# Forgetting attention and a tanh-shrink MLP on one core: another token order for q and k, and another order of the work around batch 0 and batch 1

## The chip, the cores and the metric

The kernel runs on 1 core of one Trainium2 chip. The metric is the device time of one execution in microseconds (us); lower is better. Times of runs are medians, with the lowest and the highest beside them. A profile is one execution taken by the hardware profiler; its span is the time from the first to the last instruction, which is shorter than the device time.

## What is computed

```python
# q, k, v: (8, 8, 576, 64) float32;  f: (8, 8, 576) float32;  w_in: (512, 2048);  w_out: (2048, 512)
scores = q @ k.T / sqrt(64)                       # for each batch and head
cum    = cumsum(log(clip(f, 1e-4, 1)), axis=-1)
scores = where(causal, -1e9, scores + cum[..., :, None] - cum[..., None, :])
attn   = softmax(scores)                          # with 1e-9 added to the sum
x      = (attn @ v).transpose(0, 2, 1, 3).reshape(4608, 512)
h      = x @ w_in
out    = (h - tanh(h)) @ w_out                    # (4608, 512) float32
```

## The kernel before

**Pairs.** Attention runs over 32 pairs of heads: pair p is batch p // 4, heads 2c and 2c+1 with c = p % 4. For each pair the scores are made transposed (keys in partitions, queries along the free side) in seven tiles, named s0 to s6: s0, s1, s2 of the first head, s3 a small tile for the last 64 tokens of both heads, s4, s5, s6 of the second head. A tile is some matmuls into one of two PSUM buffers (`ps_sc`) and one exponential on ScalarE that writes fp16 (`scores`, L260 on). The values of a pair (`values`, L300: 30 matmuls of 65 columns, then a reciprocal and a multiply on VectorE into `xn`) come one pair later, and `turn` (L324) puts the result transposed into `XR`: for batch 0 by TensorE and an eviction, later by a DMA transpose.

**Decay in the matmul.** QT and KT hold 64 rows of q or k and three rows more, in which the cumulated decay stands as a high and a low fp16 part, so that one matmul over 67 rows gives score plus decay. The three rows are written by DMA from the tiles `cc` and `cqs` (`load_aug`, `const_rows`, on SyncE's queue). For s0 and s1 of the very first pair the kernel doesn't wait for that: the variable `direct` takes 64 rows and adds the decay by two more matmuls with the selectors `pick_k` and `pick_q`.

**The mask.** In batch 0 (`early`) the causal mask is one more matmul per diagonal block (`neg16`, `tri16`, L281). From batch 1 on it is an affine select on GpSimd after the exponential (L297), which the values wait for.

**q and k.** Batches 0 to 2 are loaded by `load_qk` with token 6p+n in partition p (96 partitions), transposed on TensorE (`trans`, six transposes of 96 columns for a pair) into a PSUM buffer, and copied out by VectorE (L248), or ScalarE for the first q (L246). From batch 3 on other code does this with DMA transposes.

**Queues.** All loads go through GpSimd's queue in the order in which they are written; `LOADS[(p, ti)]` puts loads behind tile `ti` of pair p. GpSimd runs its queue in order, masks and load issues alike. Small SBUF copies, transposes and stores go through SyncE. All engines run in the order that the program gives them (`manual_schedule`).

**The MLP.** 9 units of 512 tokens, 32 steps each: 16 of `mlp1` (four matmuls of 512 columns, a tanh on ScalarE, an add on VectorE) and 16 of `mlp2` (four matmuls; every fourth step an eviction and a store). Its PSUM buffers are three (`ps_m`), which the transposes of batch 0 share. Pairs 0 to 3 hold no steps. Pair 4 has 3, pairs 5 to 9 have 7 each, all later ones 8; what is left runs behind the last pair.

**Order of the first pairs.** Written out by hand in BEGIN (pair 0), ORDER (1 to 3) and THEN (4): `s` a score tile, `q0` `k0` `q1` ... the transposes for the pair that many ahead, `va` `vb` the values of each head of the pair before, `x` its turn, `h` three quarters of an mlp1 step's matmuls, a bare number so many matmuls that only keep TensorE busy (`spin`), `go` the place from which the steps are spread. From pair 5 on, q's transposes for the next pair stand behind s0, values and turn behind s1, and k's transposes behind s3.

Of the kernel before, what the change touches and what calls it, by code (L numbers as in the profile page):

```python
# [8 lines left out]
FP32 = mybir.dt.float32  # L9
# [5 lines left out]
PITCH = 640  # L15
# [7 lines left out]
def kernel(  # L23
# [31 lines left out]
    aex = ctx.enter_context(tc.tile_pool(name="aex", bufs=10))  # L55
# [67 lines left out]
    pick_k = cst.tile([P, 512], FP16)  # L123
    pick_q = cst.tile([P, P], FP16)
# [4 lines left out]
    EL = [cst.tile([P, 192], FP16, tag=f"el{i}", name=f"el{i}") for i in range(3)]  # L129
    nc.vector.memset(id16, 0.0)  # L130
# [5 lines left out]
    nc.vector.memset(minus16, -1.0)  # L136
    nc.vector.memset(neg16, 0.0)
    nc.vector.memset(tri16, 0.0)
    nc.gpsimd.affine_select(out=neg16, in_=neg16, compare_op=ALU.not_equal,
# [3 lines left out]
    for i in range(2):  # L143
        nc.vector.memset(KT[i][:, :, S:PITCH], 0.0)
    nc.vector.memset(pick_k, 0.0)
    nc.vector.memset(pick_q, 0.0)
    nc.vector.memset(cqs[NH:P, :], 0.0)
    nc.vector.tensor_scalar(out=lf, in0=lf, scalar1=0.0001, scalar2=1.0,
                            op0=ALU.max, op1=ALU.min)
    nc.scalar.activation(out=lf, in_=lf, func=AF.Ln)  # L150
    nc.vector.memset(pick_k[0:1, :], -1.0)
    nc.vector.memset(pick_q[0:1, :], 1.0)
    first = cst.tile([1, 1], FP32)
    nc.scalar.activation(out=first, in_=lf[0:1, 0:1], func=AF.Exp)
    cum = cst.tile([NH, S], FP32)
# [3 lines left out]
    nc.scalar.activation(out=cq, in_=cum, func=AF.Copy, bias=-SHIFT * inv_qscale, scale=inv_qscale)  # L159
    nc.vector.scalar_tensor_tensor(out=clo, in0=cum, scalar=inv_qscale, in1=chi,  # L160
                                   op0=ALU.mult, op1=ALU.subtract)
    nc.vector.memset(pick_k[NH:NH + 1, :], -1.0)

    def load_aug(b):
        i, h0 = b % 2, b * H
        nc.sync.dma_start(out=KT[i][D:D + 1, :, 0:S], in_=chi[h0:h0 + H, :])
        nc.sync.dma_start(out=QT[i][D + 2:D + 3, :, :], in_=cq[h0:h0 + H, :])
        nc.sync.dma_start(out=KT[i][D + 1:D + 2, :, 0:S], in_=cc[NH + h0:NH + h0 + H, :])

    def const_rows(i):  # L170
        nc.sync.dma_start(out=QT[i][D:D + 2, :, :], in_=minus16)
        nc.sync.dma_start(out=KT[i][D + 2:D + 3, :, 0:S], in_=ones16[0:H, :])

    const_rows(0)
    load_aug(0)
    const_rows(1)
    load_qk(qn, q, 0, 4, H)
    load_qk(kn, k, 0, 4, H)
    for e in EL:
        nc.gpsimd.memset(e, 0.0)  # L180
    for i in range(2):
        nc.gpsimd.memset(vn[i][D:P, NJ - 1, :, :], 0.0)
        nc.gpsimd.memset(vn[i][:, :, :, D:VW], 1.0)
    load_v(0)
# [5 lines left out]
    def load_wout(t0, t1):  # L190
# [3 lines left out]
    LOADS = {(0, 0): [lambda: load_qk(qn, q, 1, 0, 2), lambda: load_qk(kn, k, 1, 0, 2),  # L194
                      lambda: load_win(0, DFF // 2)],
             (0, 3): [lambda: load_qk(qn, q, 1, 2, H), lambda: load_qk(kn, k, 1, 2, H)],
             (1, 0): [lambda: load_v(1)],
             (1, 3): [lambda: load_win(DFF // 2, DFF)],
             (2, 0): [lambda: load_wout(0, NFT // 2)],
             (3, 0): [lambda: load_wout(NFT // 2, NFT)],  # L200
             (NPAIR, 5): [lambda: load_qk(qn, q, 2, 0, H)],
             (NPAIR, 6): [lambda: load_qk(kn, k, 2, 0, H)]}
    for b in range(2, B):
        p0 = (b - 1) * NPAIR
        for n in range(NJ - 1):
            LOADS.setdefault((p0 + 1, n), []).append(lambda b=b, n=n: load_v_block(b, n, 0, H))
        LOADS.setdefault((p0 + 1, 4), []).append(lambda b=b: load_v_rest(b))
        LOADS.setdefault((p0, 0), []).append(lambda b=b: load_aug(b))
# [19 lines left out]
    def trans(b, c, src, dst, early, eng, by_head=False):  # L228
        pn, g3 = S // NT6, NT6 // 2
        if early:  # L230
            t32 = ps_m.tile([P, UW], FP32, tag="m", name="t32")
        else:
            t32 = ps_tr.tile([P, UW], FP32, tag="tr", name="t32")
        t16 = t32.bitcast(FP16)[:, 0:2 * S // 2].rearrange("p (a g n) -> p a g n", a=2, g=g3)
        for a in range(2):
            for g in range(g3):
                nc.tensor.transpose(out=t16[:, a, g, :],  # L237
                                    in_=src[b % 2][:, 2 * c + a, 2 * g:2 * g + 2, :],
                                    identity=id16[0:pn, 0:pn])
        for a0, an in ((0, 1), (1, 1)) if by_head else ((0, 2),):  # L240
            for e in range(2):
                h0 = 2 * c + a0
                to = dst[b % 2][0:D, h0:h0 + an, e:S:2].rearrange("d a (p g) -> d a p g", g=g3)
                of = t16[e * D:(e + 1) * D, a0:a0 + an, :, :].rearrange("d a g p -> d a p g")
                if eng == "A":
                    nc.scalar.activation(out=to, in_=of, func=AF.Copy)  # L246
                else:
                    nc.vector.tensor_copy(out=to, in_=of)  # L248

# [10 lines left out]
    def scores(b, c, ti, early):  # L260
# [7 lines left out]
        for a, j, i0, n, col in TILES[ti]:  # L268
            h = 2 * c + a
            edge = min(P, n) if early and i0 == j * P else 0  # L270
            direct = (b, c) == (0, 0) and ti < 2
            rows = D if direct else D + 3
            nc.tensor.matmul(out=ps[:, col:col + n], lhsT=KT[b % 2][0:rows, h, j * P:(j + 1) * P],  # L273
                             rhs=QT[b % 2][0:rows, h, i0:i0 + n], start=True, stop=not (edge or direct))
            if direct:
                nc.tensor.matmul(out=ps[:, col:col + n], lhsT=cc[:, j * P:(j + 1) * P],
                                 rhs=pick_k[:, 0:n], start=False, stop=False)
                nc.tensor.matmul(out=ps[:, col:col + n], lhsT=pick_q,
                                 rhs=cqs[:, i0:i0 + n], start=False, stop=not edge)
# [44 lines left out]
    def turn(b, c):  # L324
        xn = XN.pop((b, c))
        r0 = b % 4 * S
        if b == 0:
            x32 = ps_m.tile([P, UW], FP32, tag="m", name="x32")
# [4 lines left out]
            if c == NPAIR - 1:  # L333
                nc.vector.tensor_copy(out=XR[:, c, r0:r0 + S], in_=xt)
            else:
                nc.scalar.activation(out=XR[:, c, r0:r0 + S], in_=xt, func=AF.Copy)
# [43 lines left out]
    BEGIN = ["8", "q0", "k0", "3", "q1", "2", "s0", "k1", "s1", "s2", "s4", "s5", "q2", "s6", "s3"]  # L380
    ORDER = ["s0", "va", "s1", "vb", "s2", "k1", "s3", "2", "s4", "x", "s5", "q2", "1", "s6"]
    THEN = ["s0", "va", "vb", "s1", "s2", "h0", "h1", "x", "q1", "s3", "go", "s4", "k1", "s5", "s6"]

    def att_items(p):
# [12 lines left out]
        if p <= NPAIR:  # L397
            for what in BEGIN if p == 0 else ORDER if early else THEN:
# [4 lines left out]
                elif what == "go":  # L403
                    items.append((None, False))
                elif kind in "qk":
                    if early and p + int(arg) > NPAIR:
                        continue
                    first = p == 0 and arg == "0"
                    put(trans, *pairs[p + int(arg)], *((qn, QT) if kind == "q" else (kn, KT)), early,
                        "A" if first and kind == "q" else "V", first)  # L410
                elif kind == "v":
                    put(values, *before, (0,) if arg == "a" else (1,), not early)
                elif kind == "x":
# [6 lines left out]
        for ti in range(len(TILES)):  # L420
# [3 lines left out]
            if ti == 0 and after and after[0] < FAR:  # L424
                put(trans, *after, qn, QT, early, "V")
# [3 lines left out]
            if ti == 3 and after and after[0] < FAR:  # L429
                put(trans, *after, kn, KT, early, "V")  # L430
# [4 lines left out]
    with tc.manual_schedule(engines={PE, mybir.EngineType.Pool, mybir.EngineType.SP, mybir.EngineType.DVE,  # L435
                                     mybir.EngineType.Activation}):
        for p in range(len(pairs) + 1):
            if p == 0:
                load_aug(1)
# [4 lines left out]
            given, n, first = 0, 0, 0  # L444
            for emit, counts in items:
                n += counts
                if emit is None:
                    first = n
            whole, n = n, 0
            for emit, counts in items:  # L450
                if emit is not None:
                    emit()
                n += counts
                while n > first and (given + 1) * (whole - first) <= (n - first) * len(mine):
# [33 lines left out]
```

## Time and profile before

| | us |
|---|---|
| median of 3 runs | 365.0 |
| lowest, highest | 363.95, 365.87 |
| span of the profiled execution | 359.3 |
| the profiled execution's own time | not listed |
| TensorE, VectorE, ScalarE, GpSimd busy | 346.5, 199.1, 221.7, 153.6 |

A line of a group names source line, engine, operation, output and inputs, shapes and count; then busy time and the mean of one in ns; then the engine's idle time before them and what ended it. A line of a timeline or of the chain begins with the start in us and a duration. A line of stretches has the stretch, its length, busy time of PE (matmul), PEld (weight load), DVE (VectorE), ACT (ScalarE) and POOL (GpSimd), each with a count, and then the granted TensorE clock, the DMA share and GB/s. A line of a DMA issue ends with the median time from issue to landing. Busy time of TensorE is modelled at the end of a matmul and overlaps.

### The profile page before, as it was taken

What the parts mean: (1) busy time and instruction counts of PE and PEld (TensorE: products, weight loads), DVE (VectorE), ACT (ScalarE), POOL (GpSimd) and SP (SyncE); (2) the same over time, 40 slices, a digit from 0 to 9 for tenths busy, and PEclk for the clock granted to TensorE, in tenths of its full rate; (3) what the DMA queues carried; (4) which work ended last, traced back from release to release, by engine and by line L of the source; (5) the groups of instructions that cost most, each with busy time, mean ns of one, the idle gap of its engine ahead of it and who ended that gap; (6) DMA issues with size and microseconds to landing.
All of it is one profiled execution on the core that took longest, in us unless ns stands there. A gap on an engine that the chain in (4) does not pass through costs nothing.

```text
span 359.3 us, 7490 instructions
## 1 busy us (share of the span) xinstructions
PE 346.5 (96%) x2792; PEld 190.3 (53%) x2792; DVE 199.1 (55%) x349; ACT 221.7 (62%) x416; POOL 153.6 (43%) x316
## 2 busy tenths in 40 slices
PE   7797899999999999999999999999999999999995
PEld 3475455555555555555557865555555554444442
DVE  8666799448961577157814781378127513802710
ACT  6567676558855785578657865686568734714611
POOL 8932463766276627762776267632222210000000
PEclk9789999999999999999999999999999999999999
DMA  7999999999799999999899969991220021011011
GB/s 118 158 188 187 208 194 80 118 145 161 96 102 151 168 97 76 149 181 112 66 144 153 143 65 147 151 156 35 76 75 16 18 77 61 0 60 58 0 48 71
DMA packets 140632, 38.74 MB, mean 108 GB/s; under 512 B 128004, under 2 KB 134900, under 8 KB 140596
## 3 DMA queue, kind: packets, MB, share of 16 engines
q0 software_dynamic: 92320, 18.36, 66.7%
q1 hardware_dynamic: 48276, 19.90, 29.2%
q8 instruction: 22, 0.36, 0.4%
q14 instruction: 14, 0.11, 0.1%
HBM read 36.85 MB, written 9.44 MB: 129 GB/s over the span
## 4 chain that ended last, share of the span: by engine, by line
PE 89%; DVE 6%; ACT 2%; DMA 1%; issue 1%; ACTq 0%
PE ops L370 35%; PE hps L352 32%; PE ps L273 12%; PE av L308 8%; ACT e L287 1%; DVE gt L362 1%; DVE QT L248 1%; DMA QT<-cqs 1%; PE t L237 1%; DVE xn L320 1%; PE ps L281 1%; DVE KT L248 0%; PE spin L226 0%; DVE cum L156 0%; ACT th L359 0%
## 5 line engine op out<-in xcount | busy, mean ns | idle before, releaser
L352 PE MATMUL hps<-XR,win 128*128 128x512 f16 (+1 forms) x640 | 140.9, 357 | 0.3 <-DVE gt L362 0.2
L370 PE MATMUL ops<-wout,gt 128*128 128x512 f16 x576 | 139.2, 378 | 0.0
L287 ACT ACTIVATE e<-ps 128x512 f16<-128x512 f32 x192 | 111.0, 596 | 39.6 <-PE ps L273 26.2
L362 DVE TENSOR_TENSOR gt<-hps,th 128x512 f16<-128x512 f32 x144 | 98.5, 689 | 58.4 <-ACT th L359 57.2
L297 POOL TENSOR_SCALAR_AFFINE_SELECT e<-e 128x128 f16<-128x128 f16 x168 | 56.6, 338 | 120.8 <-ACT e L287 120.5
L359 ACT ACTIVATE th<-hps 128x512 f32<-128x512 f32 x144 | 86.3, 599 | 33.0 <-PE hps L352 31.3
L352 PEld LDWEIGHTS <-win 128*128 128x128 f16 x640 | 57.9, 97 | 48.6 <-issue 0.7
L273 PE MATMUL ps<-QT,KT 67*128 67x64 f16 (+5 forms) x384 | 77.9, 281 | 3.9 <-ACT e L287 2.1
L370 PEld LDWEIGHTS <-gt 128*128 128x128 f16 x576 | 52.0, 97 | 52.6
L273 PEld LDWEIGHTS <-KT 67*128 67x128 f16 (+1 forms) x384 | 37.7, 99 | 41.2 <-issue 2.8
L374 ACT ACTIVATE ost<-ops 128x512 f32<-128x512 f32 x36 | 21.5, 597 | 54.3 <-PE ops L370 45.3
L318 DVE TENSOR_SCALAR rs<-av 128x10 f32<-128x10 f32 (+1 forms) x33 | 5.4, 163 | 69.3 <-PE av L308 69.3
L308 PEld LDWEIGHTS <-e 128*128 128x128 f16 x896 | 32.8, 98 | 7.5 <-issue 1.7
L308 PE MATMUL av<-vn,e 128*128 128x65 f16 x896 | 34.5, 194 | 1.0 <-DVE xn L320 1.0
L106 POOL DMA_DIRECT2D vn<-in_v_dram x32 | 28.4, 898 | 1.6 <-issue 0.8
L320 DVE TENSOR_TENSOR xn<-av,rs 128x640 f16<-128x640 f32 (+1 forms) x33 | 26.5, 804 | 1.1
L248 DVE COPY KT<-t 64x576 f16<-64x576 f16 (+1 forms) x26 | 19.5, 748 | 4.5 <-PE t L237 4.3
L87 POOL DMA_DIRECT2D qn<-in_q_dram x25 | 21.5, 859 | 0.8 <-issue 0.6
L87 POOL DMA_DIRECT2D kn<-in_k_dram x25 | 21.2, 850 | 1.1 <-issue 0.9
L248 DVE COPY QT<-t 64x576 f16<-64x576 f16 x22 | 17.6, 801 | 6.5 <-PE t L237 6.3
L308 PE MATMUL av<-vn,el 128*128 128x65 f16 x64 | 12.5, 195 | 0.0
L95 DVE COPY KT<-TK 64x1152 f16<-64x1152 f16 x20 | 11.4, 607 | 0.1
(58 smaller groups left out, 127.2 us busy)
## 6 DMA issues: line engine op xcount, KB each, us to landing
out_dram<-ost SPq DMA_DIRECT2D x36, 256.0 KB
vn<-in_v_dram POOLq DMA_DIRECT2D x32, 128.0 KB, 5.9
qn<-in_q_dram POOLq DMA_DIRECT2D x20, 128.0 KB, 3.7
kn<-in_k_dram POOLq DMA_DIRECT2D x20, 128.0 KB, 4.4
win<-in_moe_w_in_dram POOLq DMA_DIRECT2D x2, 1024.0 KB, 11.8
wout<-in_moe_w_out_dram POOLq DMA_DIRECT2D x2, 1024.0 KB, 17.4
XR<-xn SPq DMA_TRANSPOSE x56
qn<-in_q_dram POOLq DMA_DIRECT2D x1, 576.0 KB, 8.9
```

The costliest lines, as they stand in the source:

```text
L87: nc.gpsimd.dma_start(out=dst[b % 2][0:pn, n, :].rearrange("p (h d) -> p h d", h=H), in_=src[b, :, n * P:n * P + pn, :].rearrange("h p d - ...
L106: nc.gpsimd.dma_start(out=vn[b % 2][:, n, h0:h1, 0:D], in_=v[b, h0:h1, n * P:(n + 1) * P, :].rearrange("h p d -> p h d"))
L248: nc.vector.tensor_copy(out=to, in_=of)
L273: nc.tensor.matmul(out=ps[:, col:col + n], lhsT=KT[b % 2][0:rows, h, j * P:(j + 1) * P], rhs=QT[b % 2][0:rows, h, i0:i0 + n], start=True, ...
L287: nc.scalar.activation(out=e[:, lo:hi], in_=ps[:, lo:hi], func=AF.Exp, scale=qscale)
L297: nc.gpsimd.affine_select(out=view, in_=view, compare_op=ALU.is_ge, fill=0.0, base=0, pattern=pat, channel_multiplier=-1)
L308: nc.tensor.matmul(out=av[:, a, ib, :], lhsT=E.pop((b, c, a, j, ib)), rhs=vn[b % 2][:, j, 2 * c + a, 0:D + 1], start=(j == 0), stop=(j == ib))
L320: nc.vector.tensor_tensor(out=xn[:, :, h0 * D:(h0 + hn) * D].rearrange("p i (a d) -> p a i d", a=hn), in0=av[:, h0:h0 + hn, :, 0:D], in1=r ...
L352: nc.tensor.matmul(out=hps[:, o:o + n], lhsT=win[:, ci, ft * P:(ft + 1) * P], rhs=XR[:, ci, t:t + n], start=(ci == 0), stop=(ci == NCH - 1))
L359: nc.scalar.activation(out=th, in_=hps, func=AF.Tanh, scale=-1.0)
L362: nc.vector.tensor_tensor(out=gt, in0=hps, in1=th, op=ALU.add)
L370: nc.tensor.matmul(out=ops, lhsT=GT[(u, ft)][:, m * P:(m + 1) * P], rhs=wout[:, ft, :], start=(ft == 0), stop=(ft == NFT - 1))
```

## The change

Six things are altered.

1. `load_qk` puts token 96n+p into partition p, so it reads pieces of 64 floats where it read 384. `trans` writes QT and KT in runs of 96 neighbouring elements where it wrote every second element.
2. All score tiles of head 0 of batch 0 are `direct`, with one 2-column tile `pick` broadcast as the selector. The DMA rows of decay are written for heads 1 to 7 at first (`const_rows(0, 1, H)`, `load_aug(0, 1)`), and head 0's constant rows in pair 4. The copy of `cq` on ScalarE stands behind the first two evictions of q (`cum_q`).
3. Fills and copies move between engines: the fills of `vn` from GpSimd to VectorE, the turns of batch 0 all to VectorE and to the buffer `ps_tr`, and batch 1's fills and rows into pair 0 (`later_rows`).
4. Loads: batch 0's q and k go in four parts each, v ahead of the last of them. The first-layer weights go in four parts behind them, in pairs 0 and 1. Batch 1's heads 0 to 3 follow in pairs 2 and 3 with the second-layer weights between; batch 1's v is in pair 4 behind s1, heads 4 to 7 of its q and k in pair 4 behind s4, and batch 2's q and k behind s6.
5. The order of pairs 0 to 4 is written in ORDERS. Pairs 1 to 3 have no spins. In pair 4 the values, three `h`, the turn and four steps (`m`) come ahead of batch 1's first transposes and scores; the pair holds 13 steps.
6. Pairs 5 to 8 have 5 steps, later ones 8.

```diff
     def load_qk(dst, src, b, h0, h1):
         nc.gpsimd.dma_start(
-            out=dst[b % 2][:, h0:h1, :, :].rearrange("p h n d -> p h (n d)"),
-            in_=src[b, h0:h1, :, :].rearrange("h (p n) d -> p h (n d)", n=NT6))
+            out=dst[b % 2][:, h0:h1, :, :].rearrange("p h n d -> p (h n) d"),
+            in_=src[b, h0:h1, :, :].rearrange("h s d -> (h s) d").rearrange("(m p) d -> p m d", p=S // NT6))
...
-    LOADS = {(0, 0): [lambda: load_qk(qn, q, 1, 0, 2), lambda: load_qk(kn, k, 1, 0, 2),
-                      lambda: load_win(0, DFF // 2)],
-             (0, 3): [lambda: load_qk(qn, q, 1, 2, H), lambda: load_qk(kn, k, 1, 2, H)],
-             (1, 0): [lambda: load_v(1)],
-             (1, 3): [lambda: load_win(DFF // 2, DFF)],
-             (2, 0): [lambda: load_wout(0, NFT // 2)],
-             (3, 0): [lambda: load_wout(NFT // 2, NFT)],
-             (NPAIR, 5): [lambda: load_qk(qn, q, 2, 0, H)],
-             (NPAIR, 6): [lambda: load_qk(kn, k, 2, 0, H)]}
+    QW = DFF // 4
+    LOADS = {(0, 3): [lambda: load_win(0, QW), lambda: load_win(QW, 2 * QW)],
+             (1, 3): [lambda: load_win(2 * QW, 3 * QW), lambda: load_win(3 * QW, DFF)],
+             (2, 3): [lambda: load_qk(qn, q, 1, 0, 2), lambda: load_qk(kn, k, 1, 0, 2)],
+             (3, 3): [lambda: load_wout(0, NFT // 2), lambda: load_qk(qn, q, 1, 2, 4),
+                      lambda: load_qk(kn, k, 1, 2, 4), lambda: load_wout(NFT // 2, NFT)],
+             (NPAIR, 1): [lambda: load_v(1)],
+             (NPAIR, 4): [lambda: load_qk(qn, q, 1, 4, H), lambda: load_qk(kn, k, 1, 4, H),
+                          lambda: const_rows(0, 0, 1)],
+             (NPAIR, 6): [lambda: load_qk(qn, q, 2, 0, H), lambda: load_qk(kn, k, 2, 0, H)]}
...
-                to = dst[b % 2][0:D, h0:h0 + an, e:S:2].rearrange("d a (p g) -> d a p g", g=g3)
-                of = t16[e * D:(e + 1) * D, a0:a0 + an, :, :].rearrange("d a g p -> d a p g")
+                to = dst[b % 2][0:D, h0:h0 + an, 0:S].rearrange("d a (g e p) -> d a g e p", g=g3, e=2)[:, :, :, e, :]
+                of = t16[e * D:(e + 1) * D, a0:a0 + an, :, :]
...
-            direct = (b, c) == (0, 0) and ti < 2
-            rows = D if direct else D + 3
+            direct = b == 0 and h == 0
...
-    BEGIN = ["8", "q0", "k0", "3", "q1", "2", "s0", "k1", "s1", "s2", "s4", "s5", "q2", "s6", "s3"]
-    ORDER = ["s0", "va", "s1", "vb", "s2", "k1", "s3", "2", "s4", "x", "s5", "q2", "1", "s6"]
-    THEN = ["s0", "va", "vb", "s1", "s2", "h0", "h1", "x", "q1", "s3", "go", "s4", "k1", "s5", "s6"]
+    BEGIN = ["8", "q0", "k0", "3", "s0", "q1", "s1", "k1", "s2", "s4", "s5", "q2", "r", "s6", "s3"]
+    ORDERS = [BEGIN,
+              ["s0", "s1", "k1", "s2", "va", "s3", "vb", "s4", "q2", "s5", "x", "s6"],
+              ["s0", "va", "s1", "vb", "s2", "k1", "s3", "s4", "x", "s5", "s6"],
+              ["s0", "va", "s1", "vb", "s2", "s3", "s4", "x", "s5", "s6"],
+              ["va", "vb", "h0", "h1", "h2", "x", "m", "m", "m", "m", "q0", "m", "k0", "m", "m", "m",
+               "s0", "m", "s1", "m", "q1", "s2", "m", "s3", "m", "k1", "s4", "s5", "m", "s6"]]
...
-            take = 0 if p < NPAIR else 3 if p == NPAIR else 7 if p <= 2 * NPAIR + 1 else 8
+            take = 5 if p <= 2 * NPAIR else 8
```

More of the change, by code (lines that the diff above doesn't have):

```diff
@@ L142 @@
                             fill=BIG, base=0, pattern=[[1, P]], channel_multiplier=-1)
[L143 to L149, printed above, removed]
     nc.scalar.activation(out=lf, in_=lf, func=AF.Ln)
-    nc.vector.memset(pick_k[0:1, :], -1.0)
-    nc.vector.memset(pick_q[0:1, :], 1.0)
     first = cst.tile([1, 1], FP32)
     nc.scalar.activation(out=first, in_=lf[0:1, 0:1], func=AF.Exp)
-    cum = cst.tile([NH, S], FP32)
+    nc.vector.memset(vn[0][D:P, NJ - 1, :, :], 0.0)
+    nc.vector.memset(vn[0][:, :, :, D:VW], 1.0)
     nc.vector.tensor_tensor_scan(out=cum, data0=ones16[0:NH, :], data1=lf, initial=0.0,
@@ L327, in turn @@
         if b == 0:
-            x32 = ps_m.tile([P, UW], FP32, tag="m", name="x32")
+            x32 = ps_tr.tile([P, UW], FP32, tag="tr", name="x32")
             xt = x32.bitcast(FP16)[:, 0:S]
@@ L397, in att_items @@
         if p <= NPAIR:
-            for what in BEGIN if p == 0 else ORDER if early else THEN:
+            for what in ORDERS[p]:
                 kind, arg = what[0], what[1:]
```

126 lines of the change are left out of this document (72 added, 54 removed).

## The prediction

> **What bounds the kernel now.** I read the page first, then the busy time by stretches, then TensorE's timeline and the chain of waits up to 62 us, and last Pool's queue.
>
> ```profile
> PE 346.5 (96%) x2792; PEld 190.3 (53%) x2792; DVE 199.1 (55%) x349; ACT 221.7 (62%) x416; POOL 153.6 (43%) x316
> PEclk9789999999999999999999999999999999999999
> 10.00:15.00 5.00, 3.25 (x31) 2.05 (x30) 3.29 (x5) 2.54 (x5) 5.00 (x8) 0.91 2.07 151
> 15.00:20.00 5.00, 4.53 (x53) 3.68 (x51) 2.12 (x5) 2.29 (x5) 5.00 (x7) 0.50 1.22 164
> 60.00:70.00 10.00, 10.00 (x93) 5.65 (x92) 5.71 (x11) 5.42 (x11) 6.83 (x14) 1.00 0.75 80
> ```
>
> The stretches list PE, PEld, DVE, ACT and POOL busy time, then the granted clock. From 60 us on PE has no idle time; before that it has, and from about 14 to 21 us it ran at half clock. So only two things count: when PE becomes full, and how much PE work is left then. The marks for this are these rows.
>
> ```profile
> 13.21 0.38 PE L273 MATMUL ps<-QT,KT 67*128 67x512 f16 x1
> 16.50 0.58 PE L273 MATMUL ps<-QT,KT 67*128 67x512 f16 x1 [0.47 <-ACT e L287]
> 23.32 0.38 PE L273 MATMUL ps<-QT,KT 67*128 67x512 f16 x1 [0.34 <-ACT e L287]
> 28.24 0.38 PE L273 MATMUL ps<-QT,KT 67*128 67x512 f16 x1 [0.37 <-ACT e L287]
> 33.54 0.47 PE av L308 x15
> 60.47 0.38 PE L273 MATMUL ps<-QT,KT 67*128 67x512 f16 x1
> 69.32 0.38 PE L273 MATMUL ps<-QT,KT 67*128 67x512 f16 x1
> 61.11 0.86 PE ops L370 x4
> 62.20 0.91 PE av L308 x30
> 25.29 0.26 PE t L237 x6
> ```
>
> Pair 1 begins at 16.50, pair 2 at 23.32, pair 3 at 28.24, the values that open pair 4's stretch at 33.54, pair 7 at 60.47, pair 8 at 69.32. An MLP step (four 512-column matmuls) takes 0.865 us, a pair's values 0.91, a set of six transposes 0.26. A full pair with seven steps takes 8.85; a pair with five therefore 8.85 - 2 x 0.865 = 7.12. By 60.47 the old kernel has done pairs 0 to 6 and 3 + 7 + 7 = 17 steps. The whole sum is: when has the new one done as much?
>
> The span is 359.3 us and the median of the runs 365.0. The profiled execution's own time is not listed, so I make the sum on the span and carry the 5.7 us between them over unchanged.
>
> **Part 1, the head and pairs 1 to 3: 2.9 to 5.0 us gained.**
>
> ```profile
> 8.06 4.42 DMA QT<-cqs
> L246 ACT ACTIVATE QT<-t 64x288 f16<-64x288 f16 x4 | 1.9, 484 | 0.0
> L287 ACT ACTIVATE e<-ps 128x512 f16<-128x512 f32 x192 | 111.0, 596 | 39.6 <-PE ps L273 26.2 <-PE ps L281 5.8 <-POOL e L297 5.6
> L287 ACT ACTIVATE el<-ps 128x128 f16<-128x128 f32 x32 | 8.8, 276 | 4.0 <-PE ps L273 3.9 <-PE ps L281 0.2
> L336 ACT ACTIVATE XR<-x 128x576 f16<-128x576 f16 x3 | 1.9, 645 | 0.0
> ```
>
> The old head waits until 12.48 (8.06 + 4.42) for the decay rows that DMA writes, and only then issues the third tile of head 0. With selectors for all of head 0 that tile goes out before. The wait stays for head 1: its row now leaves ACT behind two evictions (2 x 0.484), some 0.65 later, so head 1's first tile moves from 13.21 to about 13.6. But one tile and its exponential (0.6) are already out of the way, and pair 1 begins at 15.7 to 16.0 and not 16.50. The extra selector matmuls (two times 576 columns at 0.865 us for 2048, 0.5 us) lie in the wait for that DMA and cost nothing; 0.5 if that wait were gone.
>
> Pairs 2 and 3 are ACT's: 6 x 0.596 + 0.276 + 0.645 = 4.5 of the 4.92 between 23.32 and 28.24. The XR eviction (0.645) goes to DVE, which leaves 4.25. The taken-out spins lay in ACT's time, so they give nothing themselves. Pair 1 depends on the clock.
>
> ```profile
> 10.80:14.20 3.40, 1.66 (x13) 0.93 (x12) 2.52 (x4) 1.39 (x3) 3.40 (x6) 0.99 2.20 148
> 38.10:41.50 3.40, 1.78 (x16) 1.08 (x16) 2.77 (x5) 1.74 (x5) 0.59 (x2) 1.00 1.24 209
> 12.87 0.30 PE L273 MATMUL ps<-QT,KT 67*128 67x320 f16 x1 [1.34 <-DMA QT<-cqs]
> ```
>
> Pair 1 has 3.5 us of matmuls (scores 1.37, which is 8.85 less seven steps, the values and two sets of transposes; values 0.91, ten masks of 128 columns 0.5, two transposes of 0.26, a turn). At half clock they end at about 22.1; at full clock ACT sets 4.25 like in the others, and they end at 20.0. Two more pairs give 30.6 or 28.5 for the values now at 33.54. I take 29.6, half of the slow stretch kept: the old clock fell after the stretch with 1.66 us of PE in 3.4 and kept through the one with 1.78, and the new head has some 0.4 more than 1.66 between 10.8 and 14.2. At full clock throughout, the time comes out 1.1 lower than forecast, 366.9; a third of the main case.
>
> Here the Trainium skill (TensorE: Matmul & The Clock Gate, "Why this matters for your kernels") says that the clock halves after an idle gap of about 3 us. The trace does not agree: the longest gap before the fall at 14 is 1.34 us. By the page the new head would stay at full clock.
>
> **Part 2, pair 4: 13 steps instead of 3, all PE work that was due anyway.**
>
> ```profile
> L248 DVE COPY QT<-t 64x576 f16<-64x576 f16 x22 | 17.6, 801 | 6.5 <-PE t L237 6.3
> 38.83 0.81 DVE QT L248
> 37.34 0.29 PE x L332 x5
> L334 DVE COPY XR<-x 128x576 f16<-128x576 f16 x1 | 0.5, 458 | 1.1 <-PE x L332 1.1
> L362 DVE TENSOR_TENSOR gt<-hps,th 128x512 f16<-128x512 f32 x144 | 98.5, 689 | 58.4 <-ACT th L359 57.2
> L359 ACT ACTIVATE th<-hps 128x512 f32<-128x512 f32 x144 | 86.3, 599 | 33.0 <-PE hps L352 31.3
> ```
>
> The q and k evictions write with stride 2 now and take 0.801; the XR copy of the same 576 elements, unit stride, takes 0.458. The new order gives unit stride in runs of 96: I take 0.46, with 0.80 as the other end. That shortens the old chain around 38.8 us, which ran over these copies.
>
> From the values of pair 3 to the end of pair 4's scores and pair 5's first tile PE has 0.91 + 13 x 0.865 + four transposes of 0.26 + the turn 0.3 + scores 1.37 and 0.2 of the next pair = 15.1. Idle: 0.6 for the XR copy, 1.2 for the first tanh and gt (0.2 + 0.60 + 0.69, less the two short steps under it), and 1.4 at k0, whose one PSUM buffer is held by q0 until gt (0.69) and two evictions (0.92) are done. Sum 18.3: PE gets to pair 5's q transposes at 29.6 + 18.3 = 47.9. The second tile of pair 4 (s1) ends 13.15 after 29.6, at 42.75.
>
> **Part 3, the load that pair 5 needs: 6.8 us of waiting, the term that decides.** Those transposes read heads 4 to 7 of batch 1's q. Their load stood in pair 0; now it is queued on Pool in pair 4 behind tile s4's mask, and ahead of that, behind s1's mask, stand the five loads of batch 1's v.
>
> ```profile
> L106 POOL DMA_DIRECT2D vn<-in_v_dram x32 | 28.4, 898 | 1.6 <-issue 0.8 <-PE hps L352 0.2 <-PE ops L370 0.2
> L98 POOL DMA_DIRECT2D vn<-in_v_dram x8 | 5.7, 708 | 0.2 <-PE ps L273 0.2
> L297 POOL TENSOR_SCALAR_AFFINE_SELECT e<-e 128x128 f16<-128x128 f16 x112 | 34.0, 304 | 51.3 <-ACT e L287 51.1
> L297 POOL TENSOR_SCALAR_AFFINE_SELECT e<-e 128x256 f16<-128x256 f16 x56 | 22.7, 406 | 69.5 <-ACT e L287 69.5
> qn<-in_q_dram POOLq DMA_DIRECT2D x20, 128.0 KB, 3.7
> qn<-in_q_dram POOLq DMA_DIRECT2D x1, 288.0 KB, 5.1
> kn<-in_k_dram POOLq DMA_DIRECT2D x1, 288.0 KB, 6.6
> DMA to landing us min/median/max: 3.4/4.9/11.9
> ```
>
> s1 ends at 42.75; a tanh ahead of it, its exponential and its mask take 1.55, to 44.3; the v loads hold Pool 4 x 0.898 + 0.708 = 4.3, to 48.6; three masks (0.41 + 0.33 + 0.30) to 49.6. Then the load. The trace has loads of this size (four heads, 288 KB) at 5.1 and 6.6 from issue to landing, and 3.7 as the median of 128 KB; the last row is the fastest, middle and slowest of q's first six loads. I take 5.1, the same tensor and size: landed at 54.7. PE is in order, so nothing behind the transposes moves from 47.9 to 54.7. Queued behind it are all of pair 5's scores and values, and ACT and DVE starve with it. Ends: even with Pool free after s4's own mask, mask and 3.7 us of landing would leave 3.5; with 6.6 it is 8.3. k's load lands two or three microseconds later, when PE is still in pair 5's values and steps, and hides.
>
> **Sum.** From 54.7: the rest of pair 5, 7.12 - 0.22 = 6.9, and pair 6, 7.12, reach 68.7 with 13 + 5 + 5 = 23 steps, six more than 17 (5.2 us of work). So the old mark is reached at 63.5, against 60.47: +3.0. The tail is the same. Forecast 365.0 + 3.0 = 368.0. By the bounds: 28.5 with 3.7 gives +0.5, 30.6 with 6.6 gives +5.5.
>
> Cost nothing: the first-layer weights. Pool issues them at once behind batch 0's loads, at about 15 us.
>
> ```profile
> win<-in_moe_w_in_dram POOLq DMA_DIRECT2D x1, 1024.0 KB, 10.6
> ```
>
> The first half is then there at about 26, needed from 30.5; twice 10.6 is 36, and the fourth quarter is needed at about 46. Lateness would count in full. The later rows of decay for batch 2 on SP are needed three pairs on and cover themselves.
>
> **Rivals.** *The load lands in time (10%).* Then pair 5 runs on at 47.9 and the mark is reached at 56.7: -3.8, 361.2. It decides from a landing less than 2 us after s4's mask; the fastest of those six took 3.4, and Pool's order puts 4.3 us of v issues in front. In its favour: the 18.3 us of pair 4 are worked out by hand, and PE could be late for other reasons that hide the wait.
>
> *Small pieces clog the DMA (12%).* q and k of batches 0 to 2 are read in pieces of 256 bytes and not 1536, six times as many packets.
>
> ```profile
> q0 software_dynamic: 92320, 18.36, 66.7%
> vn<-in_v_dram POOLq DMA_DIRECT2D x4, 128.0 KB, 5.2
> ```
>
> 92,320 packets held 66.7% of 16 engines' 359.3 us: 41.5 ns each. At that price a two-head load of 1152 packets takes 3.0 us, against about 1 now; the second k pair and the first scores of pair 1 would be some 3 us late, and the wait of part 3 2 us longer: 371 to 373. Against it: v blocks already come in such pieces, 1024 packets each, issued 0.9 us apart and landing with the same 5.2, so a packet costs at most 14 ns; packet times overlap.
>
> The Trainium skill (DMA: Bandwidth & Descriptors, "Specifications") wants at least 512 bytes a transfer and sees read-modify-write below it; by it this rival would hold.
>
> *No spins, so the clock falls again in pairs 2 and 3 (5%):* each would then take 6.6 and not 4.25, 372. Against it: 3.3 us of matmuls in 4.25 is more than the 1.78 in 3.4 that kept full clock.
>
> *The evictions stay at 0.80 (7%):* 0.35 more at k0 twice over, and 0.6 in pair 1: about 369.5.
>
> **Numbers.** The main case has 66%, 365.5 to 370.5. 0.5% (1.8 us) is about what a measurement of this kernel can tell. Of the main case some four fifths lie above 366.8; with the slow rivals that is 0.73 slower; 0.17 within; faster is the 10% of the load in time. For eight in ten: 364.8 to 371.0.
>
> **What would show it.** A TensorE wait of 4 to 8 us on the DMA of qn in the first pair after the 13 steps; QT evictions at 0.46; the values of pair 3 at 28.5 to 30.6; Pool's v issues straight ahead of a 288 KB qn load. I am wrong if PE shows no wait of over 2 us on that load, or if the steps before it take over 20 us.

## The result, and the profile after

The changed kernel takes 368.95 us (368.07 to 369.9, 4 runs) beside 364.48 us (363.09 to 365.87, 4 runs) for the kernel before: ratio 1.0135, 95% interval 1.0094 to 1.0177. The forecast was 368.0, that is +3.0; measured is +4.5. The profiled execution took 368.07 us with a span of 366.4, so 1.7 us lie outside the span.

Ratios leave disturbed executions out, so they can differ a little from the quotient of the medians beside them.

The page of the changed kernel: busy time, the granted clock in 40 slices of 9.2 us, the first DMA queue (packets, MB, packet time), and the share of each engine in the chain that ended last.

```profile
PE 346.3 (95%) x2787; PEld 189.6 (52%) x2787; DVE 183.1 (50%) x358; ACT 219.2 (60%) x413; POOL 162.7 (44%) x318
PEclk9899997999999999999999999999999999999999
q0 software_dynamic: 116480, 18.36, 75.3%
PE 89%; DVE 3%; ACT 2%; DMA 2%; POOL 1%; issue 1%; ACTq 0%
```

TensorE is as busy as before (346.5 then), and the span is 7.1 longer. So the difference is idle time, or time at half clock taken for busy time. The clock row has a dent in its second slice, and a deeper one in the seventh, where the old kernel had none. TensorE's timeline shows why (start, duration, instruction, then the idle time before it and what ended it); its first two rows are the first tiles of pairs 1 and 2.

```profile
15.94 0.38 PE L287 MATMUL ps<-QT,KT 67*128 67x512 f16 x1
20.59 0.38 PE L287 MATMUL ps<-QT,KT 67*128 67x512 f16 x1
29.41 0.58 PE L322 MATMUL av<-vn,e 128*128 128x65 f16 x14
31.02 0.58 PE L322 MATMUL av<-vn,e 128*128 128x65 f16 x14 [1.00 <-DVE xn L334]
34.41 0.81 PE L363 MATMUL hps<-XR,win 128*128 128x512 f16 x3 [0.55 <-DVE XR L347]
36.19 1.02 PE L363 MATMUL hps<-XR,win 128*128 128x512 f16 x4 [0.98 <-DVE gt L373]
39.55 0.41 PE L249 MATMUL t<-id,kn 96*128 96x96 f16 x6 [1.21 <-DVE QT L260]
55.38 0.66 PE L249 MATMUL t<-id,qn 96*128 96x96 f16 x6 [5.76 <-DMA qn<-in_q_dram]
56.28 1.90 PE L363 MATMUL hps<-XR,win 128*128 128x512 f16 x4
71.80 0.38 PE L287 MATMUL ps<-QT,KT 67*128 67x512 f16 x1
```

The values of pair 3 come at 29.41, 4.0 earlier than before (33.38 in the old kernel's timeline; the 33.54 of the prediction is from its chain of waits). Then TensorE stands still for 5.76 us on the load of q, and the four matmuls after it take 1.90 us and not 1.02: half clock. Pair 7 begins at 71.80 with 23 steps done. Less the six steps more (5.2, as in the prediction) that is 66.6 against 60.47: +6.1.

On Pool's timeline and in the chain of waits the load is found where it was expected: s1's mask, five loads of v, three masks not shown, the issue, and 5.22 us to its landing.

```profile
44.83 0.29 POOL L311 TENSOR_SCALAR_AFFINE_SELECT e<-e 128x128 f16<-128x128 f16 x1 [0.79 <-ACT e L301]
45.07 3.53 POOL L106 DMA_DIRECT2D vn<-in_v_dram  x4
48.57 0.72 POOL L98 DMA_DIRECT2D vn<-in_v_dram  x1
```
```profile
50.12 5.22 DMA qn<-in_q_dram
```

The stretches around the wait (columns as in the prediction: length, then busy time of PE, PEld, DVE, ACT and POOL, granted clock, DMA, GB/s) give the clock. It falls in the second stretch, while TensorE still waits, and stays at 0.50 for all of the third, although TensorE has no gap there. In finer stretches it is half from about 53.4 to 60.3: 2 us of the wait, and the first 4.9 us of work behind it.

```profile
49.60:53.00 3.40, 0.03 (x1) 0.00 (x0) 0.53 (x1) 0.79 (x2) 3.40 (x7) 1.00 1.67 106
53.00:56.40 3.40, 1.02 (x9) 0.80 (x10) 0.32 (x1) 0.00 (x0) 3.40 (x3) 0.56 2.31 148
56.40:59.80 3.40, 3.40 (x37) 2.27 (x35) 1.28 (x3) 1.20 (x2) 2.53 (x5) 0.50 2.38 152
59.80:63.20 3.40, 3.40 (x24) 1.72 (x22) 2.32 (x5) 2.19 (x5) 0.49 (x2) 0.93 3.23 153
```

The evictions fell as taken (0.46), in the groups by line:

```profile
L260 DVE COPY QT<-t 64x576 f16<-64x576 f16 x22 | 9.9, 452 | 13.6 <-PE t L249 13.5
```

### The profile page after: what moved, and what is told of

Its sections match the earlier page's. It is cut to its first block, busy times and chain, and to the rows that moved or that the text cites. A ratio compares the mean times of both kernels' runs of the same rounds, so it can differ in the third digit from the quotient of the medians.

```text
span 366.4 us, 7488 instructions
## 1 busy us (share of the span) xinstructions
PE 346.3 (95%) x2787; PEld 189.6 (52%) x2787; DVE 183.1 (50%) x358; ACT 219.2 (60%) x413; POOL 162.7 (44%) x318
## 3 DMA queue, kind: packets, MB, share of 16 engines
q1 hardware_dynamic: 48302, 19.90, 27.2%
## 4 chain that ended last, share of the span: by engine, by line
PE 89%; DVE 3%; ACT 2%; DMA 2%; POOL 1%; issue 1%; ACTq 0%
PE ops L381 33%; PE hps L363 33%; PE ps L287 12%; PE av L322 8%; ACT e L301 1%; DMA qn<-in_q_dram 1%; PE t L249 1%; DMA XR<-xn 1%; POOL vn L106 1%; DVE xn L334 1%; ACT th L370 1%; PE ps L295 0%; DVE gt L373 0%; DVE cum L173 0%; PE ps L290 0%
## 5 line engine op out<-in xcount | busy, mean ns | idle before, releaser
L287 PE MATMUL ps<-QT,KT 67*128 67x64 f16 (+4 forms) x384 | 78.6, 279 | 3.6 <-DVE KT L260 1.8
L287 PEld LDWEIGHTS <-KT 67*128 67x128 f16 x384 | 36.8, 98 | 39.2 <-issue 4.2
L260 DVE COPY QT<-t 64x576 f16<-64x576 f16 x22 | 9.9, 452 | 13.6 <-PE t L249 13.5
L260 DVE COPY KT<-t 64x576 f16<-64x576 f16 (+1 forms) x26 | 11.2, 429 | 4.3 <-PE t L249 4.1
L249 PE MATMUL t<-id,qn 96*128 96x96 f16 x72 | 5.8, 224 | 5.8 <-DMA qn<-in_q_dram 5.8
```

The lines of the kernel that those rows point to most:

```text
L287: nc.tensor.matmul(out=ps[:, col:col + n], lhsT=KT[b % 2][0:D + 3, h, j * P:(j + 1) * P], rhs=QT[b % 2][0:D + 3, h, i0:i0 + n], start=True ...
```

## The experiments

My theory after the result: the wait on the load costs its 5.8 us and, through the clock, some 2 us more, and what the rest of the change gains is less than that. The rivals: the small pieces of the new token order hold up the loads; or the selectors and the new order of pair 4 cost the time themselves.

A mark that does without what comes later in an execution is the start of pair 7 in each profile, which all variants of the changed kernel reach with the same 23 steps. In the kernel as changed it is 71.80, and 72.47 in a second profile of it (below), so differences under some 0.7 say little.

**The kernel before, once more** (unaltered).

> The kernel before, once more. In the changed kernel's runs the time lies 1.7 us above the span, so the spans of the old kernel's timed runs (363.1 to 365.9 us) should be 361.4 to 364.2, and its profile of 359.3 an execution from the fast end. Theory: this run has a span of 361 to 364.5, and what it has more than 359.3 is half clock, in another place or longer (the 1.6 us gap at 38 us is the candidate). Rival: span 359 to 360 again and some 5 us outside it, so that the two profiles may be compared as they stand, a difference of 7.1.

Measured: 362.1 us (358.82 to 365.3, 10 runs), ratio 0.9955 (0.9914 to 0.9995); span 360.5. Its waits (in total, times, longest) and its stretches from 14 to 26 us:

```profile
PE ps L273 <- DMA QT<-cqs: 2.5, 1, 2.5
14.00:20.00 6.00, 5.05 (x54) 3.98 (x55) 1.60 (x2) 3.42 (x7) 5.10 (x8) 0.63 1.42 168
20.00:26.00 6.00, 5.66 (x81) 4.29 (x79) 4.31 (x7) 4.02 (x9) 2.12 (x3) 0.81 1.20 198
```

The wait for the rows of decay is 2.5 here and was 1.34 in the profile of the prediction; half clock stands in the same stretch. So the old kernel varies by 2% without any change to it. Its span goes roughly with its mean granted clock: over these 10 executions and 30 more it is 357.1 us at 0.997 and 0.998, 359.3 to 360.5 at 0.988 and 0.990, 360.4 to 361.4 at 0.983, and 362.2 to 364.2 at 0.974. The span of 360.5 is a little under the 361 that I expected, but 1.7 us lie outside it and not the 5 of the rival. The profile that I had built on, 359.3, was near the short end: its time would be about 361.0, and not the 365.0 of the median.

**The load early.** Heads 4 to 7 of batch 1's q and k are loaded with heads 2 and 3, in pair 3.

```diff
-             (3, 3): [lambda: load_wout(0, NFT // 2), lambda: load_qk(qn, q, 1, 2, 4),
-                      lambda: load_qk(kn, k, 1, 2, 4), lambda: load_wout(NFT // 2, NFT)],
+             (3, 3): [lambda: load_wout(0, NFT // 2), lambda: load_qk(qn, q, 1, 2, H),
+                      lambda: load_qk(kn, k, 1, 2, H), lambda: load_wout(NFT // 2, NFT)],
...
-             (NPAIR, 4): [lambda: load_qk(qn, q, 1, 4, H), lambda: load_qk(kn, k, 1, 4, H),
-                          lambda: const_rows(0, 0, 1)],
+             (NPAIR, 4): [lambda: const_rows(0, 0, 1)],
```

> The changed kernel with heads 4 to 7 of batch 1's q and k loaded together with heads 2 and 3, in pair 3, and not behind tile s4 of pair 4. Theory: the 5.8 us wait goes, and the stretch at half clock behind it (some 4.3 us of work at half speed, so 2.1 us) goes with it: 368.9 becomes 360.5 to 361.5, under the kernel before. Rival 1: the wait goes alone and another load is late in its place (v, the second-layer weights, batch 2's q): 363 to 367. Rival 2: the half clock comes anyway, from the gaps in pair 4: 363.

Measured: 362.96 us (362.08 to 364.38, 10 runs), ratio 0.9987 (0.9957 to 1.0016). TensorE's timeline (lines are one less than in the changed kernel):

```profile
49.40 0.42 PE L248 MATMUL t<-id,qn 96*128 96x96 f16 x6
52.33 0.28 PE L321 MATMUL av<-vn,e 128*128 128x65 f16 x4 [0.92 <-DMA vn<-in_v_dram]
65.77 0.38 PE L286 MATMUL ps<-QT,KT 67*128 67x512 f16 x1
```

The first row is the transposes of q, now without a wait; the last row is the mark: 6.03 us earlier. The two moved loads, q and k, give back the whole loss. What comes late next is v, as the first rival had it: 1.2 us in two waits, of which the longer is shown. That is part of why it stopped short of the 360.5 to 361.5 expected, and level with the kernel before.

**q ahead of v.** The q load stands behind s1's mask and in front of the five v loads; k stays.

```diff
-             (NPAIR, 1): [lambda: load_v(1)],
-             (NPAIR, 4): [lambda: load_qk(qn, q, 1, 4, H), lambda: load_qk(kn, k, 1, 4, H),
-                          lambda: const_rows(0, 0, 1)],
+             (NPAIR, 1): [lambda: load_qk(qn, q, 1, 4, H), lambda: load_v(1)],
+             (NPAIR, 4): [lambda: load_qk(kn, k, 1, 4, H), lambda: const_rows(0, 0, 1)],
```

> The changed kernel with one load moved: batch 1's q, heads 4 to 7, ahead of the five loads of v behind s1's mask; k stays behind s4's. Theory: the landing comes 5 us earlier, the wait shrinks from 5.8 to under 1.5 us, the clock keeps full, and v's values wait little: 361.5 to 364. Rival (the DMA is the bound, not Pool's order): the wait only moves to the values or to k's transposes, 366 to 369.

Measured: 365.69 us (363.19 to 367.96, 10 runs), ratio 1.0045 (1.0011 to 1.008).

```profile
50.98 0.43 PE L248 MATMUL t<-id,qn 96*128 96x96 f16 x6 [0.87 <-DMA qn<-in_q_dram]
54.74 0.31 PE L321 MATMUL av<-vn,e 128*128 128x65 f16 x5 [0.91 <-DMA vn<-in_v_dram]
68.45 0.38 PE L286 MATMUL ps<-QT,KT 67*128 67x512 f16 x1
```

The wait on q is 0.87 instead of 5.76, and v now waits 1.8 in three pieces. The mark is 3.35 earlier. Pool's order was the cause, and part of the wait only passes on to the load that was set back: the time lies between the two expectations, and each has a share in it.

**Spins in the wait.** The load stays late; 28 matmuls that only keep TensorE busy run in the wait (`put(spin, 28)` behind s0 of pair 5).

> The changed kernel with 28 matmuls of 512 columns that only keep TensorE busy, 6.0 us at full clock, put into the wait ahead of pair 5's q transposes. The wait stays, nothing is loaded earlier. Theory (the half clock from 52.8 to 59.7 us comes from the wait and costs 2 us): 366.5 to 367.5. Rival (the half clock costs nothing, because PE is waited for by nobody there or something else is late): 368.5 to 369.5.

Measured: 367.02 us (365.93 to 369.57, 9 runs), ratio 1.0133 (1.0084 to 1.0181).

```profile
49.39 6.21 PE L238 MATMUL spin<-ones 128*128 128x512 f16 x28
55.66 0.41 PE L249 MATMUL t<-id,qn 96*128 96x96 f16 x6
55.00:60.00 5.00, 4.94 (x60) 2.98 (x59) 3.12 (x7) 2.12 (x5) 3.88 (x5) 1.00 2.41 154
69.74 0.38 PE L287 MATMUL ps<-QT,KT 67*128 67x512 f16 x1
```

The clock behind the spins is 1.00 and not 0.50, and the mark is 2.06 earlier. The spins end some 0.5 us behind the landing (issued at 50.04, 5.1 later there), so the price of half clock is a little more than 2.06: from q's transposes to the mark it is 14.08 us here (55.66 to 69.74) and 16.42 in the changed kernel (55.38 to 71.80), 2.34 apart. The second profile of the changed kernel has 16.75, the one of the ninth experiment 16.03, so 1.9 to 2.7 in three profiles. In the times of whole executions it is not shown: the median is 1.9 below the changed kernel's, which was not run beside it, but the ratios to the kernel before are 1.0135 and 1.0133.

**The changed kernel again**, beside the next three.

> The changed kernel unaltered, beside the three that follow on one chip. Theory: 368 to 369.9 as before, with a profile whose wait on the q load is 5.3 to 6.3 us and whose clock is at half for 3.4 or 6.8 us behind it. Rival: the 368.07 that was profiled was an odd execution; then another one shows the wait under 4 us or no half clock, with the same time.

Measured: 369.04 us (368.36 to 369.44, 4 runs), ratio 1.0164 (1.0113 to 1.0215).

```profile
55.72 0.66 PE L249 MATMUL t<-id,qn 96*128 96x96 f16 x6 [5.58 <-DMA qn<-in_q_dram]
55.00:60.00 5.00, 4.28 (x43) 2.96 (x44) 1.60 (x3) 1.19 (x2) 4.42 (x6) 0.50 2.38 152
72.47 0.38 PE L287 MATMUL ps<-QT,KT 67*128 67x512 f16 x1
```

The wait and the half clock behind it come again; the first execution was no odd one.

**The old order of tokens** in the changed kernel: the load and the stride-2 eviction of the kernel before, the rest as changed.

> The changed kernel with the old order of tokens in q and k of batches 0 to 2: pieces of 1536 bytes and evictions with stride 2 at 0.80 us. Theory: the pieces cost little, the short evictions win 0.35 us at each place where TensorE waits for them (k0 twice, pair 1 twice), so without them the time is 0.7 to 1.5 us above the changed kernel's, 369.5 to 370.5. Rival: the pieces of 256 bytes hold up the loads; then the four-head q load lands 1.5 us or more sooner and the time is 365.5 to 367.5.

Measured: 371.21 us (369.3 to 372.22, 4 runs), ratio 1.0218 (1.0164 to 1.0271).

```profile
40.85 0.41 PE L249 MATMUL t<-id,kn 96*128 96x96 f16 x6 [1.89 <-DVE QT L260]
41.10 4.44 PE L363 MATMUL hps<-XR,win 128*128 128x512 f16 x12
50.73 0.41 PE L249 MATMUL t<-id,kn 96*128 96x96 f16 x6 [0.75 <-DVE QT L260]
53.48 0.39 PE L287 MATMUL ps<-QT,KT 67*128 67x512 f16 x1 [0.81 <-DVE KT L260]
58.05 0.66 PE L249 MATMUL t<-id,qn 96*128 96x96 f16 x6 [4.18 <-DMA qn<-in_q_dram]
74.28 0.38 PE L287 MATMUL ps<-QT,KT 67*128 67x512 f16 x1
```

With the old pieces of 1536 bytes the load lands in 4.9 us instead of 5.2. But TensorE comes to the wait at 53.87 (58.05 - 4.18) instead of 49.62, and 2.0 of this are spent behind evictions of 0.80 us: 1.89, 0.75 and 0.81, against 1.21, none and 0.24. Another 1.7 is half clock: behind the wait of 1.89 the granted clock is 0.50 from 42 to 44 us, and the twelve matmuls of the second row take 4.44 and not 2.75. Pool's chain is 3.0 later too (the load is issued at 53.09 and not at 50.12), so the wait hides only a part. The small pieces are not the cause of the loss; without the new order the kernel is 2.2 slower by the medians, more than the 0.7 to 1.5 expected, which had no half clock in it.

**The new order of tokens alone**, put into the kernel before.

> The kernel before with the new order of tokens alone. Theory: 0.3 to 1.2 us below the kernel before (evictions 0.45 instead of 0.80 in the chain around 38 us): 362.1 to 363.0. Rival: 1152 packets instead of 192 for a two-head load make the first tiles of batch 0 later, 364.5 to 366.5.

Measured: 363.56 us (361.88 to 364.41, 10 runs), ratio 0.9998 (0.9966 to 1.0031). Its waits:

```profile
PE t L237 <- DMA kn<-in_k_dram: 2.4, 2, 1.4
PE av L308 <- DMA vn<-in_v_dram: 2.2, 3, 0.9
```

The time lies between the two expectations, and in sum nothing is gained: 4.6 us of waits in the first 20 us for k and v of batch 0, where both profiles of the old kernel have none on k or v; their wait on the rows of decay (1.3 and 2.5) is gone in exchange. That the pieces of 256 bytes make these loads late is likely, as nothing else about the loads was changed; it is one profile of each.

**All of batch 1's loads early.** As in the second experiment, and q and k ahead of the second-layer weights, v in pair 3 too, half of the weights in pair 4.

```diff
+             (3, 3): [lambda: load_qk(qn, q, 1, 2, H), lambda: load_qk(kn, k, 1, 2, H)],
+             (3, 4): [lambda: load_wout(0, NFT // 2)],
+             (3, 6): [lambda: load_v(1)],
+             (NPAIR, 0): [lambda: load_wout(NFT // 2, NFT)],
```

> The changed kernel with heads 2 to 7 of batch 1's q and k in one load each ahead of the second-layer weights in pair 3, v of batch 1 behind the first half of those weights, and the second half in pair 4. Theory: it is the order on the queue that counts; no wait of more than 0.5 us on q, k or v in pairs 4 to 6, 360.0 to 361.5. Rival: the DMA engines are full from 20 to 55 us whatever the order, so another load comes late in their place (the second-layer weights or v), with a wait of 1 to 3 us on it and 362.5 to 365.

Measured: 362.21 us (361.28 to 364.75, 10 runs), ratio 0.996 (0.9928 to 0.9992). TensorE waits for no load of batch 1 any more, and no other load comes late in its place; the median is still 0.7 above the 361.5 that I had put as the upper end. The profiled execution was the longest of the ten, and its reason lies in the head:

```profile
8.99 0.61 PE L287 MATMUL ps<-QT,KT 67*128 67x512 f16 x1 [1.17 <-DVE KT L260]
11.00:14.00 3.00, 3.00 (x21) 1.95 (x19) 1.82 (x4) 0.79 (x2) 3.00 (x7) 0.50 1.98 133
```

The granted clock is at half from about 9 to 22 us, longer than in any other profile here of a version of the changed kernel.

**Selectors for two tiles only.** In the changed kernel, the third tile of head 0 takes the rows by DMA again.

> The changed kernel with selectors for the first two tiles only, as before; the other tiles of head 0 wait for the rows of decay that DMA writes. Theory: TensorE waits 0.5 to 1.3 us at the third tile, the whole line moves by that and the wait on the q load stays as long: 369.5 to 370.3. Rival: the selector matmuls (two times 576 columns, about 1 us at the half speed of that stretch) stand on TensorE's path in the new head and cost as much as the wait that they replace: 368.3 to 369.2.

Measured: 369.64 us (367.49 to 372.19, 4 runs), ratio 1.0219 (1.0151 to 1.0287).

```profile
11.94 0.30 PE L284 MATMUL ps<-QT,KT 67*128 67x320 f16 x1
28.31 0.58 PE L319 MATMUL av<-vn,e 128*128 128x65 f16 x14
54.19 0.66 PE L245 MATMUL t<-id,qn 96*128 96x96 f16 x6 [5.65 <-DMA qn<-in_q_dram]
70.22 0.38 PE L284 MATMUL ps<-QT,KT 67*128 67x512 f16 x1
```

The third tile starts at 11.94 with no wait at all: the rows are issued 0.6 us earlier than in the old kernel (7.50 and not 8.06) and are there. My theory expected a wait here, and there is none. The values of pair 3 even come earlier than with all selectors, at 28.31 against 29.41 and 29.92 in the two profiles of the changed kernel. That speaks for the rival, a cost of the selector matmuls; but this is the shortest of four executions, its first tile starts 0.34 earlier, and its head gets up to full pace sooner. The spread of 4.7 us doesn't let the medians speak. Whether the selectors for all of head 0 bring anything stays open. They are not the cause of the loss: the wait on q is the same.

**Another order of pair 4**, on top of the early loads: `q0` moved from behind the fourth step to the front, ahead of `va`.

> The version with batch 1's loads early, and pair 5's q transposes put ahead of batch 0's last values in pair 4, so that k's evictions are not held by one PSUM buffer. Theory: the 1.2 us wait at k0 goes and little comes in its place: 1.0 to 1.3 below the version without it, 360.9 to 361.3. Rival: the wait moves to the first first-layer steps, which the k transposes then follow sooner or later: 362.0 to 362.6.

Measured: 366.27 us (365.08 to 367.32, 8 runs), ratio 1.0091 (1.0059 to 1.0123).

```profile
31.21 0.66 PE L249 MATMUL t<-id,qn 96*128 96x96 f16 x6 [1.12 <-DMA qn<-in_q_dram]
29.20:32.60 3.40, 2.13 (x28) 1.78 (x27) 1.13 (x3) 1.53 (x3) 2.02 (x3) 0.71 2.45 158
32.60:36.00 3.40, 2.27 (x21) 1.34 (x19) 1.93 (x7) 0.00 (x0) 0.40 (x1) 0.50 3.32 152
```

A miss on both sides. The wait at k0 is gone, but q's load is not there yet at 31 us, and in this gap of 1.12 us the clock falls to half, for some 6.8 us (about 30.6 to 37.5). The second gap, 1.13 at 33.83, lies inside that time and is not its reason. I had looked for the wait at the place that I had moved from, and not for the load at the place that I moved to.

**The same with more spins in the head**: two between q0 and k0, four instead of three behind k0.

> The version of the run before with six spins instead of three in the first pair, two between q0 and k0 and four behind k0, where TensorE is idle. Theory: the time of one kernel spreads by 3 us because in some executions the clock is at half from about 9 to 21 us; with the gap filled it is not, and the time is 359 to 360.5 with a spread of under 1.5 us. Rival: the spread does not come from that gap, or six spins delay the first tile by 0.3 us: within 0.5 us of the version without them, with the same spread.

Measured: 366.27 us (366.17 to 366.41, 4 runs), ratio 1.0103 (1.0057 to 1.0149). The time didn't fall, as the rival had it. In its profile the wait on q is 1.62 and not 1.12, so what the spins do by themselves can't be told from this order. The spread of 0.24 us is small, but of four runs only.

**The early loads with these spins**, in the order of the changed kernel.

```diff
-    BEGIN = ["8", "q0", "k0", "3", "s0", ...
+    BEGIN = ["8", "q0", "2", "k0", "4", "s0", ...
```

> The version with batch 1's loads early and the old order of pair 4, with six spins instead of three in the first pair (two between q0 and k0, four behind k0). Theory: the wait on the loads and the half clock behind it are gone, and the spins keep most of the half clock out of the first 20 us: 360.5 to 361.8, below the kernel before (about 363.5) by 0.5 to 0.8%. Rival: the clock of the head doesn't hang on these gaps: 362.0 to 363.0, as without the spins.

Measured: 360.8 us (360.17 to 363.82, 12 runs) beside 362.94 us (359.45 to 366.46, 17 runs) for the kernel before, ratio 0.9952 (0.9923 to 0.9981).

```profile
8.99 0.39 PE L287 MATMUL ps<-QT,KT 67*128 67x512 f16 x1 [1.31 <-DVE KT L260]
65.04 0.38 PE L287 MATMUL ps<-QT,KT 67*128 67x512 f16 x1
```

It is the fastest version and beats both kernels: 8 us below the changed one, with which it was not run side by side, and 0.5% below the kernel before, with which it was. The first tile runs at 0.39 and not 0.61, and the mark is 6.76 before that of the changed kernel. But in this profile the half clock of the head is only moved: it stands from about 15.2 to 18.5 us, and the values of pair 3 come at 29.23, against 29.34 in the second experiment's profile without these spins. The version without the spins, 362.21, was not run beside it either, so the gain of 1.4 is not shown.

## Why the prediction came out right

The forecast of slower, the size within 1 us, and the mechanism, TensorE waiting on the q load that stands behind v on Pool's queue, are right. Two errors in the sum went against each other: the size owes something to luck.

- **The load wait (part 3): right.** Forecast 6.8, measured 5.76 and 5.58; the issue at 50.12 against 49.6, landing 5.22 against 5.1. The wait is shorter than forecast because TensorE was later, not because the load was sooner. The second experiment shows that this load is the loss: with it and k's moved, the ratio goes from 1.0135 to 0.9987.
- **The head (part 1): right in size, wrong in its reason.** Pair 3's values come at 29.41 against 29.6, and pair 1 begins at 15.94, within the 15.7 to 16.0 forecast. From there I had kept half of the old slow stretch. The trace has none of it: the granted clock is 1.00 from 15.94 to 29.41, and half clock stands at 9 to 12.3 instead. What made up for it is that pair 1 takes 4.65 and pair 2 4.59 (20.59 to 25.18), not 4.25. So the 29.6 was luck in part. (My end at half clock doesn't follow from my own terms either: twice 3.5 us from 15.85 on would be 22.9, and not 22.1.) And the ninth experiment has the rows in time without the selectors, so the early third tile, which I gave the gain to, is not needed for it.
- **Pair 4 (part 2): 1.9 us short.** TensorE stood before the load at 49.62 (55.38 - 5.76), 20.2 after the values of pair 3 and not 18.3. The three idle times that I had named are 0.55, 0.98 and 1.21 against 0.6, 1.2 and 1.4. Missed is the one between the two heads' values, 1.00 for VectorE's multiply that frees their PSUM, and some more matmul time than the 15.1 summed up. It cost nothing here, as it fell into the wait; without the wait it counts. My own sign of being wrong, steps that take over 20 us, is just met.
- **Behind the wait: the mis-sized term.** "The rest of pair 5, 6.9, and pair 6, 7.12" from the landing to pair 7 makes 14.0 at full clock; measured 16.42 (55.38 to 71.80). The 2.4 missing are the half clock: the fourth experiment has the same work at full clock in 14.08. I had forecast a gap of 6.8 us, and had seen the clock fall behind a gap of 1.34 in the same trace, and still put the work behind it at full clock.
- **The sum on one profile: wrong base.** I made the sum against a span of 359.3 and carried 5.7 us over as fixed. Outside the span lie 1.7; the other 4 were the distance of that execution from the median. Profile to profile the change costs 7.1 (359.3 to 366.4), by medians 4.5. At the old mark it is +6.1 where +3.0 was forecast: 0.65 of the difference because the load landed at 55.34 and not at 54.7, 2.4 behind it. The last 1.0 of the 7.1 comes behind the mark, and I have not traced it. That the forecast is within 1 us of the median is owed in part to the old profile being a short execution, which I didn't know.
- **The rivals.** *The load lands in time* was priced at -3.8 at the old mark; the second experiment makes it so, and its mark of 65.77 less 5.2 is 60.6, +0.1. Of the 3.9 missing, 1.5 are pair 4's, which now count (TensorE begins the transposes at 49.40 and not at 47.9). Another 1.9 are v's lateness: the two heads' values of pair 4 start 2.34 apart (50.96 and 53.30), and 0.45 in the fourth experiment, which has no wait on v. The idle times before them give only 1.2 of this, as modelled busy times overlap. The other 0.5 I could not place. *Small pieces clog the DMA* falls for the changed kernel: undone, the time goes up by 2.2, and the load lands in 4.9 instead of 5.2 us. *The clock falls again in pairs 2 and 3* falls: the page's clock row has no dent there. *The evictions stay at 0.80* falls with 0.452; its price was put at 1.5, and the old order as a whole costs 2.2, with a half clock that I had not counted.

On the clock, the Trainium skill (TensorE: Matmul & The Clock Gate, "Why this matters for your kernels") sees the throughput drop behind idle gaps of more than about 3 us. The wait of 5.76 us with 0.50 behind it agrees, and the rule would have pointed to the missing term. The tenth experiment, with the same fall in a gap of 1.12 us, doesn't agree, nor does the sixth, with a fall behind 1.89: shorter gaps can be enough. (The longest gap of 1.34 us that the prediction names leaves out 1.67 us ahead of the first matmul.) My own reading in the prediction, that the clock fell behind 1.66 us of matmuls in 3.4 and kept behind 1.78, doesn't hold as a rule: in the tenth experiment it fell at 30.6, behind 2.23 us of matmuls from 27.2 to 30.6, and in the changed kernel it kept behind 2.15 in the same stretch. What makes it fall stays open.

## What to carry to other kernels

Of a moved load, add up what its queue holds in front of it: here five issues of v, 4.2 us on Pool, stood ahead of a load that takes 5.2, and TensorE waited 5.8; with the load ahead of v it was 0.9. A wait on TensorE costs more than its length where the clock falls with it. Here the fall lasted 6.9 us, of which 4.9 were work, and cost 2.3 us; see whether spins in the gap or a load in another place is to be had. Before a sum is set against one profile, ask where that execution stands among the runs: the span of each run tells. The granted clock is only a hint: four executions of the changed kernel have spans of 366.4 to 367.7 at 0.986 and 368.2 at 0.991.

## What was not expected of the hardware

- The fall of the clock lasts: it begins about 3.8 us into the wait of 5.76 us and ends 4.9 us behind it, though TensorE had no gap there, at a price of 2.34 us. In the tenth experiment it lasts as long, some 6.8 us, from a gap of 1.12.
- The granted clock doesn't tell the pace everywhere. In the fifth experiment's profile the matmuls between 8.99 and 13.5 us start at the same times as in the eighth's (0.40 to 0.43 apart for 512 columns, about twice the 0.22 of full pace), but the row of this stretch shows 1.00, where the eighth has 0.50:

```profile
8.00:14.00 6.00, 5.52 (x34) 3.15 (x33) 3.31 (x9) 2.42 (x5) 6.00 (x10) 1.00 2.00 133
```

- Pool's issue of a load grows with its pieces: the four-head load takes 1.20 us to issue in pieces of 256 bytes and 0.72 in the sixth experiment's pieces of 1536.
